# A DeltaNet plus MLP-mixer kernel: the value loads of units 6 to 23 go from SyncE's queue to GpSimd's

## The chip, the cores and the metric

The kernel runs on one core of a Trainium2 chip. The metric is the device time of one execution in microseconds (us). PE is TensorE, DVE is VectorE, ACT is ScalarE, POOL is GpSimd and SP is SyncE, as the profile names them. Every engine works through its own instructions in the order in which the program lists them; a DMA is issued by an instruction on one engine's stream, and what stands behind that instruction on that engine waits until it has been issued.

## What is computed

```python
# DeltaNet, for each of B=4 batches and H=8 heads, S=768 steps, D=48
k_n = k / (norm(k) + 1e-6)
for t in range(S):
    y[t]  = q[t] @ state
    v_old = state @ k_n[t]
    state = state + beta[t] * outer(k_n[t], v[t] - v_old)
x = y.transpose(0, 2, 1, 3).reshape(4, 768, 384)
# MLP mixer
h = relu(x.T @ w_tok1) @ w_tok2
u = x + h.T
out = u + relu(u @ w_ch1) @ w_ch2
```

## The kernel before, in words

The sequence of a batch is cut into 6 units of 128 steps, so there are 24 units (0 to 23, six to a batch), and each unit into two chunks of 64 steps. The recurrence is solved chunk by chunk. All eight heads of a unit are worked on together; in the stacked tiles the 128 partitions hold 64 steps of two heads that are processed side by side, and the free axis holds four such pairs, two chunks and 48 values.

For a unit `u` these jobs do the work. `load_kq(u)` (L372) loads keys and queries. `prep(u)` (L453) takes the norms of the keys, turns keys and queries, and makes two scaled tiles: `mb` (L497), the mask times the scale of every step, and the key columns of `gm` (L514); for the units from 4 on POOL makes both. `grams(u, cc)` (L434) multiplies keys with keys and queries on PE, and DVE scales the result with `mb` (L443). `to_parts`, `invert`, `from_parts` and `join` invert the triangular blocks. From unit 6 on the blocks go out to memory and back by DMA (L608, L655, L685, L633), and the inversion is a long run of small DVE operations (L661, L666). `load_v(u)` (L406) loads the values in four DMAs through `stacked` (L397), and POOL then adds a small constant to the norms (L411) and multiplies the values by them (L414), in place in tile `v_st`. `recur(t)` (L773) walks the chunks `t = 2u` and `2u + 1` in order: DVE subtracts the values from what the state gives (L797, the first and usually the only reader of `v_st`; in the first chunk of a batch PE reads `v_st` itself, L814), and the state is updated. `mixer(b)` (L979) runs the two MLPs of a batch on PE. Weights come in pieces through `round_weights` (L262): a DMA on SP (L271), two operations on ACT, one on DVE, and an addition on POOL (L284) that ends the use of one of three landing buffers `d64`.

Tile `v_st` has two buffers. A load of a new unit's values can start only when the earlier unit in its buffer has been read by L797 for the last time. In the order of the work, unit 6 takes the buffer of unit 5, unit 7 that of 4, unit 8 that of 6, unit 11 that of 9, unit 13 that of 12, unit 16 that of 14, unit 19 that of 18, unit 21 that of 19, unit 22 that of 20 and unit 23 that of 21.

The order of everything is written out by hand: a long string (from L1162) names the jobs step by step, and each word advances one job by one step, whichever engine that step uses. So `v8*2` issues two of the four loads of unit 8 at that place. The string fixes the order on each engine. Each of the four loads of a unit is a step of its own; the fifth step is L411 with L414. Read along the string, the POOL work and the value loads around five units stand in this order, where `v8.1` is the first load of unit 8, `w` an addition of L284, `mb` and `gm` L497 and L514 of a unit, and `V` L411 with L414:

- v7.1 v7.2 v7.3, w15, w4, w19, v6.1 to v6.4, V6, v7.4, w12
- w20, v8.1 v8.2 v8.3, gm12, v8.4, mb13, gm13, V8
- gm14, v11.1 v11.2 v11.3, mb15, gm15, v11.4, mb16, V11
- gm16, v14.1 to v14.4, v13.1 to v13.4, V13, mb18, gm18, V14
- mb21, v16.3 v16.4, V16, gm21 (v16.1 and v16.2 stand before gm20)
- V18, v19.1 to v19.4, V19, v21.1 to v21.4, V21, gm22, v22.1 to v22.4, v23.1, V22, v23.2 v23.3 v23.4, V23

Before the change the loads in these lists are issued by SP and the rest is POOL's; SP meets the loads between its other DMAs of keys, queries, weights, inversion blocks and results. Every DMA of the kernel is issued by SP.

Of the kernel before, what the change touches and what calls it, by code (L numbers as in the profile page):

```python
# [23 lines left out]
def kernel(  # L24
# [39 lines left out]
    nc = tc.nc  # L64
# [5 lines left out]
    NCH = S // U  # L70
# [142 lines left out]
    def place(u):  # L213
        return NV + u if u < 2 else (u - 2) % NV
# [101 lines left out]
    while rounds[-1][-1] < NU - 1:  # L316
        u = rounds[-1][-1] + 1
# [17 lines left out]
    def heads_of(src, u):  # L335

        b, c = divmod(u, NCH)
        return src[b, :, c * U : (c + 1) * U, :].rearrange(
            "(p par) (cc s) d -> par cc s p d", par=2, s=C
        )  # L340
# [31 lines left out]
    def load_kq(u):  # L372
        b, c = divmod(u, NCH)
        kst = kst_of[slot(u)]
        if u >= TU:
            yield from load_rows(u, 0, k)
            assert last_in(u) in ranked
            yield from stacked(kst, k, u)
            yield from load_rows(u, 1, q)
            return  # L380
        for pad, src in ((kpad, k), (qpad, q)):
            assert last_in(u) is None or (pad is kpad, last_in(u)) in turned
            nc.sync.dma_start(
                out=pad[slot(u)][:, :, 0:D],
                in_=src[b, :, c * U : (c + 1) * U, :].rearrange("h t d -> t h d"),
            )
            yield
            if src is k and u >= RU:
                yield from stacked(kst, k, u)

        heads = kpad[slot(u)].rearrange("t (p par) d -> t p par d", par=2)
        for cc in range(2 if u < RU else 0):
            for par in range(2):
                nc.scalar.copy(kst[PAR[par ^ cc], :, cc], heads[PAR[cc], :, par, 0:D])
                yield

    def stacked(dst, src, u):  # L397
        rows = heads_of(src, u)
        for par in range(2):
            for cc in range(2):  # L400
                nc.sync.dma_start(
                    out=dst[PAR[par ^ cc], :, cc], in_=rows[par, cc]
                )
                yield

    def load_v(u):  # L406
        vsts[u] = v_st = loads.tile([128, NP, 2, D], FP32, name="v_st")
        yield from stacked(v_st, v, u)
        assert u in masked
        nrm = nrms[place(u)]  # L410
        nc.gpsimd.tensor_tensor(  # L411
            out=nrm, in0=nrm, in1=eps[:, :, None].to_broadcast([128, NP, 2]), op=ALU.add
        )
        nc.gpsimd.tensor_tensor(  # L414
            out=v_st, in0=v_st,
            in1=nrm[:, :, :, None].to_broadcast([128, NP, 2, D]), op=ALU.mult,
        )
        scaled.add(u)
        yield
# [712 lines left out]
    for u in range(NU):  # L1132
        jobs[f"k{u}"] = load_kq(u)
        jobs[f"p{u}"] = prep(u)
        jobs[f"c{u}"], jobs[f"d{u}"] = (grams(u, cc) for cc in range(2))
        jobs[f"t{u}"] = to_parts(u)
        if u < NCH:
            jobs[f"h{u}"] = join_16(u)
        jobs[f"f{u}"] = from_parts(u)
        jobs[f"j{u}"] = join(u)  # L1140
        jobs[f"v{u}"] = load_v(u)
# [137 lines left out]
```

## Time and profile before

| what | us |
|---|---|
| median of 3 runs (639.05 to 644.09) | 641.08 |
| the profiled execution | 638.03 |
| its span in the profile | 636.3 |
| its mean granted TensorE clock, of full speed | 0.981 |
| DMA traffic read and written | 39.42 MB and 9.44 MB |

The profile is one execution. The times in its rows count from the start of the span, so 1.7 us of the profiled execution's 638.03 us lie outside it. A row of the timeline gives the start, the duration, the engine, the line of the kernel, the operation, what it writes and reads, and in brackets how long the engine had been idle before it and what ended that idle time. `SPq` is SP's queue of issues: its duration is the time in which SP was busy with issuing.

### The profile page before, as it was taken

What the parts mean: (1) busy time and instruction counts of PE and PEld (TensorE: products, weight loads), DVE (VectorE), ACT (ScalarE), POOL (GpSimd) and SP (SyncE); (2) the same over time, 40 slices, a digit from 0 to 9 for tenths busy, and PEclk for the clock granted to TensorE, in tenths of its full rate; (3) what the DMA queues carried; (4) which work ended last, traced back from release to release, by engine and by line L of the source; (5) the groups of instructions that cost most, each with busy time, mean ns of one, the idle gap of its engine ahead of it and who ended that gap; (6) DMA issues with size and microseconds to landing.
All of it is one profiled execution on the core that took longest, in us unless ns stands there. A gap on an engine that the chain in (4) does not pass through costs nothing.

```text
span 636.3 us, 21488 instructions
## 1 busy us (share of the span) xinstructions
PE 606.3 (95%) x9132; PEld 529.0 (83%) x9132; DVE 447.3 (70%) x1132; ACT 259.5 (41%) x631; POOL 108.7 (17%) x146
## 2 busy tenths in 40 slices
PE   8488798899999999999999999999999999999997
PEld 5367676667898988958999999769999987999997
DVE  4987876966899568988969987785627253373643
ACT  7758886447422242125623333135244230223240
POOL 2348364235301113021110010101010000000000
PEclk9878997899999999999999999999999999999999
DMA  9787568646442444354444033202020000000000
GB/s 201 131 145 170 138 133 206 151 111 155 104 111 60 92 110 92 81 131 79 92 103 101 13 94 49 66 10 38 2 54 2 27 2 0 26 1 26 1 26 26
DMA packets 135776, 50.27 MB, mean 79 GB/s; under 512 B 114656, under 2 KB 130144, under 8 KB 135680
## 3 DMA queue, kind: packets, MB, share of 16 engines
q1 hardware_dynamic: 135680, 48.89, 34.5%
q8 instruction: 72, 1.18, 0.8%
q14 instruction: 24, 0.20, 0.1%
HBM read 39.42 MB, written 9.44 MB: 77 GB/s over the span
## 4 chain that ended last, share of the span: by engine, by line
PE 81%; DVE 7%; ACT 5%; DMA 3%; issue 2%; SPq 1%; POOL 0%; DVEq 0%; ACTq 0%; POOLq 0%
PE p_o L1088 26%; PE p_r L958 19%; PE p_c L1066 7%; PE p L986 5%; PE p_h L999 5%; PE p_k L790 3%; PE p_s L828 3%; PE p_g L440 3%; PE p_y L810 3%; DMA d<-in_moe_w_ch_dram 1%; PE p_z L748 1%; PE p_ut L1009 1%; PE p_w L814 1%; DVE sub L661 1%; PE p_y L829 1%
## 5 line engine op out<-in xcount | busy, mean ns | idle before, releaser
L1088 PE MATMUL p_o<-wc,r 128*128 128x192 f32 x720 | 125.8, 329 | 0.6 <-ACT u_t L1013 0.6
L1088 PEld LDWEIGHTS p_o<-wc,r 128*128 128x128 f32 x720 | 116.7, 190 | 2.7 <-ACT u_t L1013 1.1
L970 DVE TENSOR_TENSOR r<-r,p_r 128x512 f32<-128x512 f32 x90 | 59.7, 684 | 39.9 <-PE p_r L958 38.8
L1017 DVE TENSOR_TENSOR xb<-xb,p_o 128x192 f32<-128x192 f32 x84 | 29.3, 350 | 59.5 <-PE p_o L1088 59.3
L967 ACT COPY r<-p_r 128x512 f32<-128x512 f32 x54 | 31.5, 584 | 91.4 <-PE p_r L958 89.8
L666 DVE TENSOR_TENSOR x<-x,sub 128x84 f32<-128x84 f32 (+24 forms) x178 | 59.6, 335 | 6.1
L661 DVE TENSOR_TENSOR sub<-x 128x84 f32<-128x84 f32 (+24 forms) x178 | 58.4, 328 | 7.1 <-DMA x<-n_dram 2.8
L1066 PE MATMUL p_c<-u_t,wc 128*128 128x256 f32 x216 | 51.2, 387 | 0.2 <-ACT u_t L1013 0.2
L1088 PE MATMUL p_o<-wc,s 128*128 128x192 f32 x288 | 50.5, 329 | 0.3 <-DVE xb L1017 0.3
L414 POOL TENSOR_TENSOR v_st<-v_st,nrm 128x384 f32<-128x384 f32 x24 | 20.6, 859 | 174.6 <-DMA v_st<-in_v_dram 140.7
L1088 PEld LDWEIGHTS p_o<-wc,s 128*128 128x128 f32 x288 | 46.8, 190 | 1.2 <-DVE xb L1017 0.6
L820 ACT COPY w_t<-p_w 128x192 f32<-128x192 f32 x48 | 15.3, 319 | 73.2 <-PE p_w L814 72.5
L1066 PEld LDWEIGHTS p_c<-u_t,wc 128*128 128x128 f32 x216 | 39.6, 190 | 5.9 <-ACT u_t L1013 0.4
L974 ACT ACTIVATE r<-r 128x512 f32<-128x512 f32 x54 | 33.8, 630 | 25.6 <-DVE r L970 25.3
L440 PE MATMUL p_g<-kq 48*64 48x128 f32 (+1 forms) x704 | 38.3, 290 | 3.3 <-ACT kq L509 3.3
L497 POOL TENSOR_TENSOR mb<-mask_c,cs 128x512 f32<-128x512 f32 x20 | 21.0, 1050 | 114.1 <-DVE gm L443 45.1
L842 ACT ACTIVATE xb<-p_y 64x192 f32<-64x192 f32 x96 | 31.1, 324 | 21.3 <-PE p_y L829 10.5
L958 PE MATMUL p_r<-u_t,wc 128*128 128x128 f32 x288 | 38.5, 277 | 0.0
L958 PE MATMUL p_r<-t_d,wc 128*128 128x128 f32 x288 | 37.2, 280 | 0.0
L443 DVE TENSOR_TENSOR gm<-p_g,mb 128x512 f32<-128x512 f32 x44 | 29.4, 683 | 10.0 <-PE p_g L440 7.2
L986 PE MATMUL p<-xb,w 128*128 128x384 f32 x96 | 35.6, 513 | 0.0
L958 PEld LDWEIGHTS p_r<-u_t,wc 128*128 128x128 f32 x288 | 35.3, 192 | 0.3
(177 smaller groups left out, 1200.1 us busy)
## 6 DMA issues: line engine op xcount, KB each, us to landing
d<-in_moe_w_ch_dram SPq DMA_DIRECT2D x24, 384.0 KB, 3.9
v_st<-in_v_dram SPq DMA_DIRECT2D x96, 48.0 KB, 2.5
out_dram<-xb SPq DMA_DIRECT2D x23, 192.0 KB, 1.9
kst<-in_k_dram SPq DMA_DIRECT2D x64, 48.0 KB, 3.2
n_dram<-gm SPq DMA_DIRECT2D x72, 32.0 KB, 2.4
pads<-in_k_dram SPq DMA_DIRECT2D x24, 96.0 KB, 2.4
pads<-in_q_dram SPq DMA_DIRECT2D x24, 96.0 KB, 2.5
gm<-w_dram SPq DMA_DIRECT2D x72, 32.0 KB, 2.1
```

The lines of the kernel that those rows point to most:

```text
L440: nc.tensor.matmul(p_g[PAR[i ^ cc], p], kqt[f, p, cc, 0], kqt[f, p, cc])
L661: nc.vector.tensor_tensor(out=tmp, in0=y[:, :, 0:s, s : s + 1].to_broadcast([n, k, s, w]), in1=y[:, :, s : s + 1, s + 1 : m].to_broadcast( ...
L666: nc.vector.tensor_tensor(out=y[:, :, 0:s, s + 1 : m], in0=y[:, :, 0:s, s + 1 : m], in1=tmp, op=ALU.add,)
L842: nc.scalar.mul(y[:, :, D * i : D * i + D], p_y[PAR[1 - i]], 1.0 if c else -1.0)
L958: nc.tensor.matmul(p[:, i], pieces[i // width][:, at : at + 128], f[f"u{n}"], start=first and i == 0, stop=True, skip_group_check=True,)
L967: nc.scalar.copy(o, p)
L970: nc.vector.tensor_tensor(out=o, in0=o, in1=p, op=ALU.add if sign > 0 else ALU.subtract)
L974: nc.scalar.activation(o, o, ACTF.Relu)
L986: nc.tensor.matmul(p_1[dh], piece_of(w1, c, 0)[:, dh * 128 : (dh + 1) * 128], xb[:, c], start=(c == 0), stop=(c == NCH - 1),)
L999: nc.tensor.matmul(p_h, piece_of(w2, j, c * 128)[:, c * 128 : (c + 1) * 128], r1[j], start=(j == 0), stop=(j == NDH - 1),)
L1066: nc.tensor.matmul(p_c[:, k], piece_of(wc1, cb, f * 128)[:, f * 128 : (f + 1) * 128], u_t[:, cb], start=(cb == 0), stop=(cb == NCB - 1),)
L1088: nc.tensor.matmul(p, a[:, m], wc2[:, m, j], start=(start and i == 0), stop=(i == NM - 1), skip_group_check=True,)
```

## The change

The helper that issues the four loads takes the queue as an argument, and `load_v` passes GpSimd's for the units from 6 on (`NCH` is 6). Keys keep SyncE. The order string is unchanged.

```diff
-    def stacked(dst, src, u):
+    def stacked(dst, src, u, queue=nc.sync):
         rows = heads_of(src, u)
         for par in range(2):
             for cc in range(2):
-                nc.sync.dma_start(
+                queue.dma_start(
                     out=dst[PAR[par ^ cc], :, cc], in_=rows[par, cc]
                 )
                 yield
 
     def load_v(u):
         vsts[u] = v_st = loads.tile([128, NP, 2, D], FP32, name="v_st")
-        yield from stacked(v_st, v, u)
+        yield from stacked(v_st, v, u, nc.sync if u < NCH else nc.gpsimd)
```

That is 18 units with four loads each, 72 of the kernel's 96 value loads. One load moves 48 KB: for 64 steps and four heads 256 rows of 48 values (192 bytes) each, from memory into 64 partitions.

## The prediction

> **What bounds the kernel now.** I read the page's busy times and its chain first, then busy time by stretch, then the waits of SP.
>
> ```profile
> PE 606.3 (95%) x9132; PEld 529.0 (83%) x9132; DVE 447.3 (70%) x1132; ACT 259.5 (41%) x631; POOL 108.7 (17%) x146
> PE 81%; DVE 7%; ACT 5%; DMA 3%; issue 2%; SPq 1%; POOL 0%; DVEq 0%; ACTq 0%; POOLq 0%
> ```
>
> ```profile
> core 0: us, PE busy (x) PEld busy (x) DVE busy (x) ACT busy (x) POOL busy (x), PEclk, DMA share, GB/s
> 105.00:140.00 35.00, 33.00 (x421) 21.94 (x422) 30.37 (x83) 13.74 (x36) 8.27 (x10) 0.92 0.59 136
> 140.00:500.00 360.00, 358.86 (x5790) 317.28 (x5784) 274.27 (x703) 131.29 (x321) 49.77 (x67) 1.00 0.33 74
> ```
>
> ```profile
> 105.59 1.31 SPq L401 DMA_DIRECT2D v_st<-in_v_dram  x2
> ```
>
> TensorE is the bound: 81% of the chain is PE's and SP's queue holds 1%. The first moved load is the second of these two issues, at 106 us; the last of all starts at 471 us (the row of L401 below). In 140 to 500 us PE is busy for 358.86 of 360 us, at full granted clock. So a gain on SP has little to be spent on. Its upper bound is the idle time there, 1.1 us, plus idle time (2.0) and lost clock (0.08 of 35, 2.8 us) in 105 to 140 us: 5.9 us, 0.9% of the time. A loss has no such bound: PE runs in a fixed order, and values or masks that come late stop it.
>
> **What the change removes from SP.**
>
> ```profile
> L401 SPq DMA_DIRECT2D v_st<-in_v_dram x96: 595/610/2146, 9.1 to 471.0; - x96
> ```
>
> ```profile
> SPq L401 <- DVE rest L797: 14.8, 2, 14.6
> SPq L271 <- POOL wc L284: 8.4, 5, 3.5
> ```
>
> 72 issues of 0.61 us (the median) are 44 us of SP's time, and 14.8 us in which SP stood before a load until the buffer of `v_st` was free. I cost this at nothing: what waits behind are loads for units and weights to come, and PE is busy meanwhile. If that cover were thinner, it would be the 5.9 us above.
>
> **What it adds to POOL.** POOL gets 72 issues. No row shows what one costs there, since POOL issues no DMA before the change. The nearest rows:
>
> ```profile
> L411 POOL TENSOR_TENSOR nrm<-nrm,eps 128x8 f32<-128x8 f32 x24 | 6.2, 257 | 0.2
> L541 POOL MEMSET z<- 128x2304 f32 x1 | 2.0, 2017 | 0.0
> ```
>
> From below: POOL's shortest work takes about 0.26 us (L411), if all it does is hand the DMA on. From above: if POOL writes the transfer out row by row, four words for each of 256 rows on each of two sides make 2048 words; at the memset's 2017 ns for 2304 elements, 0.88 ns each, that is 1.8 us, and with SP's 0.61 us as the fixed part 2.4 us. The count of four words is my assumption. If besides POOL could write only while DVE is idle (85.73 of 360 us in 140 to 500), an issue of 0.61 us would stretch to 0.61 / 0.238 = 2.6 us, and both together would go beyond 3. I call the cost of one issue d and take d = 1.2 us, twice SP's row for the same transfer and nearer to that row than to any other; the ends 0.26 and 3.0 are kept for the range. At 1.2 us the issues add 86 us to POOL's 108.7 us of work: room enough in total.
>
> The Trainium skill (DMA: Bandwidth & Descriptors, section Latency and other measured facts) gives the first byte at about 1 us through GpSimd and about 0.6 us through SP; by that difference alone an estimate of d is 1.0, and the sum below would be the same, zero. No run here shows it yet.
>
> **Which POOL work gets late.** The loads are put in POOL's own order, so what counts is each later instruction against its first use. POOL's rows, then DVE's:
>
> ```profile
> 111.14 0.83 POOL L414 TENSOR_TENSOR v_st<-v_st,nrm 128x384 f32<-128x384 f32 x1 [6.62 <-DMA lent<-in_k_dram]
> 113.86 1.03 POOL L284 TENSOR_TENSOR wc<-w_f,d 128x384 uint32<-128x384 uint32 x1 [1.90 <-ACT gm L739]
> 139.36 1.04 POOL L497 TENSOR_TENSOR mb<-mask_c,cs 128x512 f32<-128x512 f32 x1
> 158.88 1.02 POOL L284 TENSOR_TENSOR wc<-w_f,d 128x384 uint32<-128x384 uint32 x1 [2.22 <-DVE w_f L280]
> 159.86 0.83 POOL L514 TENSOR_TENSOR gm<-kst,cs 128x384 f32<-128x384 f32 x1
> 163.77 1.04 POOL L497 TENSOR_TENSOR mb<-mask_c,cs 128x512 f32<-128x512 f32 x1 [3.08 <-DVE cs L476]
> 216.47 1.04 POOL L497 TENSOR_TENSOR mb<-mask_c,cs 128x512 f32<-128x512 f32 x1 [18.46 <-DVE gm L443]
> 318.80 1.04 POOL L497 TENSOR_TENSOR mb<-mask_c,cs 128x512 f32<-128x512 f32 x1 [7.98 <-DVE gm L443]
> 326.49 0.83 POOL L414 TENSOR_TENSOR v_st<-v_st,nrm 128x384 f32<-128x384 f32 x1 [6.49 <-DMA v_st<-in_v_dram]
> 412.10 0.83 POOL L414 TENSOR_TENSOR v_st<-v_st,nrm 128x384 f32<-128x384 f32 x1 [11.57 <-DMA v_st<-in_v_dram]
> 470.81 0.83 POOL L414 TENSOR_TENSOR v_st<-v_st,nrm 128x384 f32<-128x384 f32 x1 [38.13 <-DMA v_st<-in_v_dram]
> ```
>
> ```profile
> 169.81 1.27 DVE L443 TENSOR_TENSOR gm<-p_g,mb 128x512 f32<-128x512 f32 x2
> 173.62 0.35 DVE L797 TENSOR_TENSOR rest<-p_k,v_st 128x192 f32<-128x192 f32 x1
> 214.87 0.32 DVE L797 TENSOR_TENSOR rest<-p_k,v_st 128x192 f32<-128x192 f32 x1
> 227.38 0.69 DVE L443 TENSOR_TENSOR gm<-p_g,mb 128x512 f32<-128x512 f32 x1 [0.42 <-PE p_g L440]
> 273.63 0.35 DVE L797 TENSOR_TENSOR rest<-p_k,v_st 128x192 f32<-128x192 f32 x1
> 285.66 0.36 DVE L797 TENSOR_TENSOR rest<-p_k,v_st 128x192 f32<-128x192 f32 x1
> 327.35 0.36 DVE L797 TENSOR_TENSOR rest<-p_k,v_st 128x192 f32<-128x192 f32 x1 [0.75 <-POOL v_st L414]
> 406.68 0.36 DVE L797 TENSOR_TENSOR rest<-p_k,v_st 128x192 f32<-128x192 f32 x1
> 417.93 0.31 DVE L797 TENSOR_TENSOR rest<-p_k,v_st 128x192 f32<-128x192 f32 x1
> 467.61 0.36 DVE L797 TENSOR_TENSOR rest<-p_k,v_st 128x192 f32<-128x192 f32 x1 [0.74 <-PE p_k L790]
> 474.13 0.36 DVE L797 TENSOR_TENSOR rest<-p_k,v_st 128x192 f32<-128x192 f32 x1 [0.98 <-PE p_k L790]
> ```
>
> ```profile
> v_st<-in_v_dram SPq DMA_DIRECT2D x96, 48.0 KB, 2.5
> ```
>
> A load lands 2.5 us after its issue begins; for one that takes d to issue I use 1.9 + d.
>
> - Unit 13's mask. POOL is free at 159.90 us (L284), then come three issues, L514, one issue and L497: it ends at 159.9 + 4d + 1.9 = 161.8 + 4d. First use is 169.81: safe up to d = 2.0.
> - Unit 19's values. Their buffer is free at 407.04 (end of L797). The fourth load starts 3d later and lands at 408.9 + 4d, L414 adds 0.8: 409.7 + 4d against 417.93, safe up to d = 2.0. At d = 1.2 they are 1.6 us later than now, within the 5.0 us between 412.93 and 417.93.
> - Unit 13's values, in the same way from 273.98: 276.7 + 4d against 285.66, d = 2.2.
> - Unit 16's values have no slack today: ready at 327.32, used at 327.35 after 0.75 us of DVE idle time. Two loads now follow unit 21's mask (ends at 319.84): 322.6 + 2d, at d = 1.2 2.3 us earlier than today; later than today only from d = 2.4. Gain on DVE 0.75 us, on the busy PE nothing.
> - Unit 15's mask stands behind three loads of unit 11, whose buffer is free at 215.19 (end of L797 at 214.87): 216.2 + 3d against 227.38, d = 3.7.
> - Unit 23's first load takes POOL's place for over 20 us, until 467.97, with unit 22's L414 behind it. That still ends at 469.0 + d plus 0.2, against a first use at 474.13.
> - The weight addition at 113.86 now follows three loads that start when unit 5's L414 ends, at about 112.0: it starts at 112.0 + 3d, 1.7 us late at d = 1.2. SP waits for its end today before it issues a further weight load (its waits on L284 above), so SP and the key and query loads behind it move by those 1.7 us, less what SP saves on three issues. What is loaded there serves units 11 and 12, whose masks come at 139.36 us and later.
>
> The sum at d = 1.2: nothing is added to PE's path and nothing taken. The profiled execution's 638.03 us stay; it lies 3.05 us below the median of 641.08, and the forecast is for a median: **641 us**.
>
> **Rivals.**
>
> *An issue is dear (slower).* Place: the stretches above; price by their terms; it decides from d = 2.0. At 2.4 us: unit 13's mask is 1.6 late, unit 19's values 1.4, unit 13's values 0.6, together 3.6 us, 645. At 3.0 us: 4.0, 3.8 and 3.0 us, plus unit 16 with 1.2 against its first use and 2.2 us for unit 8 (its L414 stands behind the late mask and two more POOL steps, about 2.0 us, and ends at 163.8 + 4d against 173.62): 14 us, 655. For it: 256 short rows each. Against it: POOL's software does not make it slow elsewhere: L497 takes 1.04 us for the 128x512 elements for which DVE's L443 takes 0.69.
>
> The Trainium skill (SBUF — State Buffer, section SBUF: two separate sides) says that a DMA issued by GpSimd starves while DVE holds the port pair that both share, and gives (section A bandwidth-pool intuition that's wrong) 620 ns alone and 3100 ns beside a DVE copy. As an estimate by that figure d would be 3.1, and this rival's price a little above 14 us. The same page (Who interferes with whom) ties this to DVE's copies and tensor-scalar forms; whether its starving comes in here, no run yet shows.
>
> *DVE is held (slower).* POOL's work already slows DVE:
>
> ```profile
> 411.38 0.39 DVE L666 TENSOR_TENSOR x<-x,sub 64x234 f32<-64x234 f32 x1
> 412.25 0.94 DVE L666 TENSOR_TENSOR x<-x,sub 64x238 f32<-64x238 f32 x1
> ```
>
> The second ran beside L414 at 412.10 and took 0.55 us more. If each of 72 issues does this, DVE loses up to 40 us; DVE's idle time in 140 to 500 us is 85.73 us, so a good part goes unseen. I put a quarter of it on the path: 10 us, 651.
>
> *SP's relief pays (faster).* The earlier loads feed PE's idle time and lift the clock in 105 to 140 us: at most 5.9 us, 635. Against it: at the first moved loads PE is idle for 2.0 of 35 us, and the work before 106 us keeps its queue.
>
> **How the numbers follow.** No change 0.45 (641, own range 638 to 645); dear issue 0.33; DVE held 0.14; relief 0.08. A measurement of this kernel can tell about 1% from no change, 6.4 us. The dear issue stays within that in 0.03, DVE held in 0.01 and relief in 0.03: faster 0.05, same 0.45 + 0.07 = 0.52, slower 0.43. The range goes from 636.5 (most of the relief) to 657 (issues of 3.0 us and a little more); outside lie about 0.03 below, and above 0.12 of the dear issue and 0.03 of DVE held.
>
> **What would show it.** POOL's rows: 72 issues of about 1.2 us; 2.0 or more speaks for the first rival. Unit 13's L443 still near 169.8 and unit 19's L797 near 417.9: right; PE idle there, waiting for L414 or L443: wrong. The longer forms of L661 and L666 at more than 0.4 us beside issues speak for the second rival; PE's clock above 0.92 in 105 to 140 us for the third. The forecast is wrong if PE's busy share of 140 to 500 us falls by more than 6 us.

## The result, and the profile after

| | median us | runs | lowest to highest |
|---|---|---|---|
| before | 641.12 | 20 | 637.66 to 645.17 |
| after | 644.82 | 20 | 639.92 to 650.62 |

The ratio is 1.0045, with a 95% interval of 1.0024 to 1.0066. The changed kernel is 3.7 us by the medians, 2.9 by the ratio, slower; little, but clear of zero. The forecast of no change (641) lies inside the measured spread but outside the interval: something was lost that the prediction priced at nothing.

Two of the 20 runs after, 649.81 us and the first profiled execution with 650.62 us, lie more than 1.5% above the fastest and are left out of the ratio. All rows "after" below are of a second profiled execution of the same kernel (`again`, 646.12 us, span 644.4). The first has the same three stops of PE: it is busy for 17.53, 37.33 and 38.67 us of the last three stretches shown below.

What answers to the bound first: the page's busy times, then busy time by stretch. After the start and the length of a stretch stand the busy time and instruction count of PE, PE's loads, DVE, ACT and POOL, the granted clock, the DMA share and the traffic.

```profile
PE 611.8 (95%) x9132; PEld 531.2 (82%) x9132; DVE 451.1 (70%) x1132; ACT 259.8 (40%) x631; POOL 153.1 (24%) x218
...
PE 75%; DVE 11%; ACT 4%; DMA 4%; issue 3%; SPq 3%; POOL 1%; DVEq 0%; ACTq 0%; POOLq 0%
```

```profile
105.00:140.00 35.00, 32.89 (x403) 21.60 (x402) 30.75 (x84) 13.59 (x35) 12.34 (x18) 0.90 0.59 136
140.00:500.00 360.00, 354.27 (x5740) 311.31 (x5739) 276.26 (x698) 131.76 (x321) 89.94 (x132) 1.00 0.33 75
```

PE's share of the chain falls from 81% to 75%, DVE's rises from 7% to 11%, and in 140 to 500 us PE is busy for 354.27 us instead of 358.86. The 4.6 us that are missing lie in a few places. The same view in shorter stretches, before and then after:

```profile
140.00:180.00 40.00, 39.31 (x848) 33.39 (x842) 30.61 (x73) 24.06 (x61) 15.13 (x18) 1.00 0.58 138
180.00:200.00 20.00, 20.00 (x160) 17.91 (x159) 18.79 (x51) 2.71 (x5) 3.21 (x6) 1.00 0.43 100
260.00:300.00 40.00, 40.00 (x641) 30.68 (x639) 35.27 (x99) 12.81 (x34) 5.43 (x7) 1.00 0.38 89
300.00:340.00 40.00, 39.60 (x778) 37.09 (x773) 32.02 (x80) 15.73 (x39) 5.67 (x8) 1.00 0.48 105
```

```profile
140.00:180.00 40.00, 38.83 (x829) 32.31 (x828) 27.56 (x65) 23.24 (x57) 20.44 (x26) 0.96 0.57 130
180.00:200.00 20.00, 18.43 (x167) 16.29 (x166) 16.22 (x46) 2.57 (x7) 6.46 (x10) 1.00 0.40 102
260.00:300.00 40.00, 38.46 (x507) 29.04 (x507) 35.92 (x103) 9.45 (x27) 6.32 (x10) 1.00 0.37 86
300.00:340.00 40.00, 38.59 (x886) 36.08 (x883) 33.66 (x70) 19.15 (x48) 13.03 (x19) 1.00 0.44 92
```

Three stops of PE, of 1.57, 1.54 and 1.01 us, make 4.1 of the 4.6 us. They are called by their place in the first profile of the kernel before, near 182, 282 and 325 us; in `again` they end at 186.94, 288.89 and 333.71 us. The 0.5 us in 140 to 180 us are no loss of the change: two more profiles of the kernel before have 38.73 and 39.11 us there. Nor is the shift of some 3 us with which the rows after 160 us begin: in the same two profiles the L443 of 169.81 us stands at 174.26 and 173.21.

The issues themselves are cheap. The first row is POOL's group by line (count, then busy us and mean ns, then idle time and its releasers); the others are of the DMA view (packets, MB, share of the DMA engines; KB each, median us from issue to landing).

```profile
L401 POOL DMA_DIRECT2D v_st<-in_v_dram x72 | 44.9, 630 | 118.0 <-DVE rest L797 53.0 <-DVE sub L661 44.7 <-DVE t_c L927 15.9
```

```profile
q0 software_dynamic: 2304, 3.54, 3.0%
...
v_st<-in_v_dram POOLq DMA_DIRECT2D x72, 48.0 KB, 2.7
```

An issue takes 0.63 us on POOL, against 0.61 on SP, and lands after 2.7 us, against 2.5.

**The stop near 282 us.** POOL, then DVE, after:

```profile
279.67 2.46 POOL L401 DMA_DIRECT2D v_st<-in_v_dram  x4 [22.04 <-DVE sub L661]
...
284.58 0.83 POOL L414 TENSOR_TENSOR v_st<-v_st,nrm 128x384 f32<-128x384 f32 x1 [2.23 <-DMA v_st<-in_v_dram]
285.37 1.07 POOL L497 TENSOR_TENSOR mb<-mask_c,cs 128x512 f32<-128x512 f32 x1
286.40 0.83 POOL L514 TENSOR_TENSOR gm<-kst,cs 128x384 f32<-128x384 f32 x1
...
287.47 0.83 POOL L414 TENSOR_TENSOR v_st<-v_st,nrm 128x384 f32<-128x384 f32 x1
```

```profile
281.05 0.36 DVE L666 TENSOR_TENSOR x<-x,sub 128x198 f32<-128x198 f32 x1
...
284.63 0.91 DVE L666 TENSOR_TENSOR x<-x,sub 128x108 f32<-128x108 f32 x1
285.57 0.97 DVE L661 TENSOR_TENSOR sub<-x 128x84 f32<-128x84 f32 x1
286.58 0.75 DVE L666 TENSOR_TENSOR x<-x,sub 128x84 f32<-128x84 f32 x1
```

and the same place before:

```profile
282.07 0.83 POOL L414 TENSOR_TENSOR v_st<-v_st,nrm 128x384 f32<-128x384 f32 x1 [28.28 <-DMA v_st<-in_v_dram]
```

```profile
275.96 0.37 DVE L666 TENSOR_TENSOR x<-x,sub 128x198 f32<-128x198 f32 x1
...
279.52 0.27 DVE L666 TENSOR_TENSOR x<-x,sub 128x108 f32<-128x108 f32 x1
279.83 0.25 DVE L661 TENSOR_TENSOR sub<-x 128x84 f32<-128x84 f32 x1
...
281.48 0.21 DVE L666 TENSOR_TENSOR x<-x,sub 128x30 f32<-128x30 f32 x1
```

Beside the four issues of POOL (279.67 to 282.13 us) DVE runs at its usual pace: the 128x198 form takes 0.36 us, before 0.37. Beside the four arithmetic steps it does not: 0.91 and 0.97 us instead of 0.27 and 0.25. Before, POOL began these steps at 282.07, after the inversion's last operation (281.48 and 0.21), because unit 13's values had landed only then. SP had come to their loads at 277.72 us, 3.7 us after L797 had freed the buffer (273.98); POOL comes to them 0.6 us after the same L797 (279.08). Now they land while the inversion still runs. A load that arrives sooner has let POOL's arithmetic in beside DVE's, and PE waits for what stands behind it on DVE (`[1.54 <-DVE xb L1003]` at PE's next L999).

DVE operations that read one input from PSUM are not held: over the whole of `again` L443, which reads `p_g`, takes 0.65 to 0.69 us, and L797, which reads `p_k`, 0.31 to 0.36 us, beside POOL's arithmetic or not.

The Trainium skill (SBUF — State Buffer, section Who interferes with whom) says that a DVE instruction with two inputs in SBUF contends with a GpSimd instruction that reads SBUF, and not with one that only writes there. The rows above agree with the first half (0.91 us against 0.27). No run here tests the second half: no row shows whether POOL reads or writes SBUF while it issues a DMA.

**The stop near 325 us** is of the same kind: unit 16's L414 and unit 21's L514 stand beside the weight forms of L927.

```profile
330.18 0.85 POOL L414 TENSOR_TENSOR v_st<-v_st,nrm 128x384 f32<-128x384 f32 x1 [1.86 <-DMA v_st<-in_v_dram]
330.99 0.88 POOL L514 TENSOR_TENSOR gm<-kst,cs 128x384 f32<-128x384 f32 x1
```

```profile
330.06 0.28 DVE L927 TENSOR_TENSOR t_c<-u_t,t_c 128x128 f32<-128x128 f32 x1
330.26 0.91 DVE L927 TENSOR_TENSOR t_d<-t_d,u_t 128x128 f32<-128x128 f32 x1
331.10 0.91 DVE L927 TENSOR_TENSOR t_d<-u_t 128x128 f32<-128x128 f32 x1
```

**The stop near 182 us** is another thing: DVE waits for the blocks of the next inversion, which go to memory by the writes of L608 and come back by the read of L655. After:

```profile
186.21 0.19 DVE L661 TENSOR_TENSOR sub<-x 128x30 f32<-128x30 f32 x1 [2.67 <-DMA x<-n_dram]
```

and before:

```profile
180.16 0.20 DVE L661 TENSOR_TENSOR sub<-x 128x30 f32<-128x30 f32 x1
```

Before, there was no wait, but no slack either: the read had landed at 179.96 us.

### The profile page after: what moved, and what is told of

It reads as the page before. It is cut to its first block, busy times and chain, and to the rows that moved or that the text cites. A ratio compares the mean times of both kernels' runs of the same rounds, so it can differ in the third digit from the quotient of the medians.

```text
span 648.8 us, 21509 instructions
## 1 busy us (share of the span) xinstructions
PE 615.4 (95%) x9132; PEld 534.5 (82%) x9132; DVE 452.2 (70%) x1132; ACT 259.7 (40%) x631; POOL 152.2 (23%) x218
## 3 DMA queue, kind: packets, MB, share of 16 engines
q0 software_dynamic: 2304, 3.54, 2.8%
HBM read 39.42 MB, written 9.44 MB: 75 GB/s over the span
## 4 chain that ended last, share of the span: by engine, by line
PE 73%; DVE 12%; DMA 6%; ACT 4%; issue 3%; SPq 1%; POOL 1%; DVEq 0%; POOLq 0%; ACTq 0%
PE p_o L1088 22%; PE p_r L958 20%; PE p_c L1066 7%; PE p_h L999 5%; PE p L986 3%; PE p_k L790 3%; DVE x L666 3%; DVE sub L661 3%; PE p_s L828 3%; PE p_y L810 3%; PE p_g L440 3%; DMA x<-n_dram 2%; DMA n_dram<-gm 1%; PE p_z L748 1%; PE p_w L814 1%
## 5 line engine op out<-in xcount | busy, mean ns | idle before, releaser
L1088 PE MATMUL p_o<-wc,r 128*128 128x192 f32 x720 | 127.9, 332 | 3.9 <-DVE xb L1017 3.3
L401 POOL DMA_DIRECT2D v_st<-in_v_dram x72 | 44.6, 626 | 119.7 <-DVE rest L797 52.0
L661 DVE TENSOR_TENSOR sub<-x 128x84 f32<-128x84 f32 (+24 forms) x178 | 60.9, 342 | 12.4 <-DMA x<-n_dram 8.1
L666 DVE TENSOR_TENSOR x<-x,sub 128x84 f32<-128x84 f32 (+24 forms) x178 | 60.7, 341 | 6.1
L820 ACT COPY w_t<-p_w 128x192 f32<-128x192 f32 x48 | 15.2, 317 | 80.9 <-PE p_w L814 80.1
L497 POOL TENSOR_TENSOR mb<-mask_c,cs 128x512 f32<-128x512 f32 x20 | 21.1, 1053 | 95.8 <-DVE cs L476 35.7
L999 PE MATMUL p_h<-r,w 128*128 128x384 f32 x96 | 34.1, 508 | 1.9 <-DVE xb L1003 1.9
L443 DVE TENSOR_TENSOR gm<-p_g,mb 128x512 f32<-128x512 f32 x44 | 29.3, 681 | 8.9 <-PE p_g L440 7.3
```

What stands on the lines that cost most here:

```text
L401: queue.dma_start(out=dst[PAR[par ^ cc], :, cc], in_=rows[par, cc])
L661: nc.vector.tensor_tensor(out=tmp, in0=y[:, :, 0:s, s : s + 1].to_broadcast([n, k, s, w]), in1=y[:, :, s : s + 1, s + 1 : m].to_broadcast( ...
L666: nc.vector.tensor_tensor(out=y[:, :, 0:s, s + 1 : m], in0=y[:, :, 0:s, s + 1 : m], in1=tmp, op=ALU.add,)
L999: nc.tensor.matmul(p_h, piece_of(w2, j, c * 128)[:, c * 128 : (c + 1) * 128], r1[j], start=(j == 0), stop=(j == NDH - 1),)
L1088: nc.tensor.matmul(p, a[:, m], wc2[:, m, j], start=(start and i == 0), stop=(i == NM - 1), skip_group_check=True,)
```

## The experiments

Except where a diff is shown, a kernel is the changed one with another condition in the one line of `load_v`:

```diff
-        yield from stacked(v_st, v, u, nc.sync if u < NCH else nc.gpsimd)
+        yield from stacked(v_st, v, u, nc.sync if u < NCH or u in (9, 10) else nc.gpsimd)
```

`sp_` names the units that go back to SP, `pool_` those that alone are POOL's. `again` is the changed kernel, `before_2` and `before_3` are the kernel before. Ratios are to the kernel before on the same chip, of 12 runs each (`twice` 6), with 95% intervals. The profiled execution of `pool_6_10` took 648.95 us, the longest of its twelve. PE's busy time is of the profiled execution; "wait" is that of the first L661 after L655 near 182 us.

| kernel | wait | PE 180-200 | PE 260-300 | PE 300-340 | ratio, interval |
|---|---|---|---|---|---|
| before | 0 | 20.00 | 40.00 | 39.60 | |
| `before_2` | 0.31 | 20.00 | 40.00 | 39.44 | 1.0003, 0.9974 to 1.0031 |
| `before_3` | 1.21 | 19.91 | 40.00 | 39.42 | one run |
| `again` | 2.67 | 18.43 | 38.46 | 38.59 | 1.0046, 1.0016 to 1.0077 |
| `sp_9_10` | 4.14 | 17.00 | 37.73 | 39.28 | 1.0044, 1.0015 to 1.0073 |
| `sp_13_14` | 0.93 | 19.96 | 40.00 | 38.54 | 1.0031, 1.0000 to 1.0062 |
| `sp_9_10_13_14` | 3.82 | 17.33 | 40.00 | 38.97 | 1.0030, 1.0003 to 1.0056 |
| `sp_13_14_16` | 5.00 | 16.15 | 40.00 | 39.50 | 1.0015, 0.9982 to 1.0049 |
| `sp_6_8` | 2.13 | 19.02 | 38.60 | 39.28 | 1.0045, 1.0011 to 1.0079 |
| `sp_6_8_b` | 2.33 | 18.83 | 39.28 | 39.01 | one run |
| `pool_6_10` | 5.21 | 15.93 | 40.00 | 39.09 | 1.0011, 0.9981 to 1.0041 |
| `pool_13_14` | 2.18 | 18.97 | 39.73 | 39.12 | 1.0022, 0.9988 to 1.0056 |
| `pool_13_14_b` | 2.06 | 19.08 | 38.73 | 39.60 | one run |
| `pool_17_23` | 0.15 | 19.95 | 40.00 | 39.40 | 0.9996, 0.9964 to 1.0028 |
| `k14_pool` | 0.59 | 19.80 | 39.26 | 38.86 | 1.0023, 0.9999 to 1.0048 |
| `k14_pool_sp_13_14_16` | 0.53 | 19.80 | 40.00 | 39.48 | 0.9995, 0.9975 to 1.0014 |
| `twice` | 0 | 20.00 | 40.00 | 39.60 | 1.0078, 1.0054 to 1.0101 |

PE's busy time is not the whole price of the longest stops. Where PE is busy for 15.93 and 16.15 of the 20 us (`pool_6_10`, `sp_13_14_16`), the granted clock of that stretch is 0.83, and it is 0.91 at 17.33 us (`sp_9_10_13_14`), where `again` and `sp_9_10` have 1.00.

Two names of theories recur with another meaning from set to set; each expectation says what it means by them.

**First set: which loads make the stops near 182 and 282 us.**

> The changed kernel once more, for a second trace. Theory ROUND TRIP: taken out of SP's order, the value loads run earlier than the inversion blocks that units 10 to 17 send to memory and read back; they compete with these DMAs, DVE starts rounds 3 and 4 of the inversion late, and some of POOL's arithmetic on the values now falls into an inversion and holds DVE. Then this trace shows again: L661 idle for the landing of x<-n_dram by 2 us or more near 185 us, PE idle near 187 and near 290 us, at least three operations of L661/L666 in 285 to 295 us at 0.7 us and more, and a time about 0.45% above the kernel before (643 to 646 us). Rival STRAY: these waits belong to one disturbed execution; then PE is busy in 180 to 300 us for 119 us of 120 and the extra time lies elsewhere. Rival ISSUE: the issues themselves (0.63 us each) hold POOL or DVE; then L661/L666 are longer beside issues of L401 on POOL and mask or value steps end late.

> The loads of units 9 and 10 go back to SP, 64 of the 72 stay on POOL. ROUND TRIP: the wait of L661 for x<-n_dram near 185 us is gone (under 0.5 us) and with it the stop of PE there; the time falls by 2 to 4 us against the changed kernel, the stop near 290 us stays. ISSUE: 8 of 72 issues are gone, the time falls by at most 0.5 us. STRAY: no change that can be told.

> The loads of units 13 and 14 go back to SP. ROUND TRIP: the wait of L661 for x<-n_dram near 264 us and the long L661/L666 at the end of that inversion (near 288 us) are gone, PE does not stop there; the time falls by 2 to 4 us against the changed kernel, the stop near 187 us stays. ISSUE: at most 0.5 us less. STRAY: no change that can be told.

> The loads of units 9, 10, 13 and 14 go back to SP, 56 stay on POOL. ROUND TRIP: both stops of PE are gone, the time is that of the kernel before within 0.3% (639 to 643 us). ISSUE: 16 of 72 issues are gone, so about a fifth of the loss: some 0.3% above the kernel before is left.

The loss is there again (1.0046), and so are the stops, so STRAY fails. Taking units 13 and 14 off POOL removes the stop near 282 us in both kernels that do it (40.00 of 40 us). In `sp_13_14` POOL starts unit 13's L414 after the inversion's end again:

```profile
285.39 0.83 POOL L414 TENSOR_TENSOR v_st<-v_st,nrm 128x384 f32<-128x384 f32 x1 [31.92 <-PE p_h L999]
```

```profile
284.39 0.21 DVE L666 TENSOR_TENSOR x<-x,sub 128x30 f32<-128x30 f32 x1
```

Taking off units 9 and 10, whose loads POOL issues beside the blocks' way through memory, does not remove the stop near 182 us (4.14 and 3.82 us of waiting). So those loads are not its cause, and ROUND TRIP fails for this stop. It fails in `sp_13_14` too, where the stop should have stayed: the wait there is only 0.93 us and PE is busy 19.96 of 20 us, though none of the loads put back is issued before 250 us. Why is not known. The times of single stops, 1 to 2 us, are within the intervals, so here the windows decide, not the ratios.

**Second set: one part alone, and unit 16.**

> The kernel before once more, unchanged: a second profiled execution of it. It is there for the stop near 182 us, where the inversion's first subtraction (L661) waits for its blocks from memory. Theory FETCH: that round trip ends on time or 2 to 3 us late according to how 16 KB instruction packets fall on its writes, in any version, so it can be late here too (busy time of PE in 180 to 200 us of 17 to 20). Theory STRAY: it is late only where values are loaded by POOL, so PE is busy 20.0 of 20 here as in the first profile of the kernel before. Both: 260 to 300 us 40.0 busy, 300 to 340 us 39.5 or more. Ratio to the kernel before 1.000 with an interval of about 0.003 on either side, which is also the noise of the other comparisons.

> Only the loads of units 13 and 14 by GpSimd, all others by SyncE. Theory COLLISION: these loads alone bring the stop near 282 us, because their values land before the inversion's end and the multiplications of L414 then run beside its last steps: L661 and L666 there 0.7 us or more instead of 0.25, busy time of PE in 260 to 300 us of 38 or less, in 300 to 340 us 39.5 as before; time 1 to 3 us over the kernel before. Rival SP AHEAD (the stop needs SP to be free of the other loads): 40.0 of 40 and no change of time. Near 182 us: 20.0 busy by STRAY, anything from 17 to 20 by FETCH.

> Only the loads of units 6 to 10 by GpSimd, 11 to 23 by SyncE. COLLISION: no stop near 282 us (40.0 of 40) and none near 325 us (39.5 of 40 in 300 to 340 us); the rival SP AHEAD says the same here, since SP has 11 to 23 again. Near 182 us: STRAY expects the stop as in four of five kernels with values on POOL (17 to 18.5 of 20 in 180 to 200 us) and a time 2 us over the kernel before; FETCH leaves it open, 17 to 20.

> The change without units 13, 14 and 16, whose loads stay on SyncE. COLLISION: the stop near 282 us is gone (40.0 of 40 in 260 to 300 us) as in the kernel without 13 and 14, and so is the one near 325 us (the forms of L927 are not held, 39.5 of 40 in 300 to 340 us), because unit 16's multiplication comes later again; what is left over the kernel before is the stop near 182 us, 0 to 2.5 us. Rival: unit 21's columns (L514), not unit 16's values, hold the forms, and the time from 300 to 340 us stays at 38.5 to 39.0.

`sp_13_14_16` shows what makes the stop near 325 us: with unit 16 on SP, PE is busy 39.50 of 40 us, and L927 is never held, because unit 16's L414 comes after the forms:

```profile
333.73 1.12 POOL L414 TENSOR_TENSOR v_st<-v_st,nrm 128x384 f32<-128x384 f32 x1 [6.17 <-DMA v_st<-in_v_dram]
```

```profile
330.95 0.28 DVE L927 TENSOR_TENSOR t_d<-u_t 128x128 f32<-128x128 f32 x1
```

The other profiles agree. In the eight with unit 16 on POOL (`twice` aside, where L417 comes after the forms) one or two forms of L927 take 0.91 or 0.92 us; in the nine with unit 16 on SP none does. PE loses most where two forms are held (busy 38.54 to 38.67 of 40 us; 38.86 to 39.28 with one). `pool_6_10` and `pool_13_14` were expected at 39.5 of 40 us here and have 39.09 and 39.12, without a form held; PE waits there for ACT's L820 (0.4 us).

`pool_13_14` is the other half of the proof for 282 us: these eight loads alone bring the collision.

```profile
283.20 0.93 POOL L414 TENSOR_TENSOR v_st<-v_st,nrm 128x384 f32<-128x384 f32 x1 [2.88 <-DMA v_st<-in_v_dram]
```

```profile
283.48 0.73 DVE L661 TENSOR_TENSOR sub<-x 128x58 f32<-128x58 f32 x1
284.24 0.97 DVE L666 TENSOR_TENSOR x<-x,sub 128x58 f32<-128x58 f32 x1
```

It comes one step later in the inversion, holds fewer operations, and costs PE 0.27 us, in the second profile (`pool_13_14_b`) 1.27: less than the 2 us or more expected. How many of the last steps are caught differs from one profile to the next. `pool_6_10` has no stop near 282 us, as expected. Near 182 us it has the longest wait of all, 5.21 us, and yet `pool_13_14`, which issues nothing on POOL until 256 us, waits 2.18 us there. That does not fit STRAY, which expected no stop in `pool_13_14`; FETCH, which allowed anything, is not tested by it.

**Third set: slack for the round trip, and twice the issues.** In `k14_pool` POOL also issues the four key loads of unit 14, which SP issued between the nine writes of blocks:

```diff
-                yield from stacked(kst, k, u)
+                yield from stacked(kst, k, u, nc.gpsimd if u == 14 else nc.sync)
```

The same edit stands at the other place where these loads are issued. In `twice` each load on POOL is cut into two halves of its pairs:

```diff
-                queue.dma_start(
-                    out=dst[PAR[par ^ cc], :, cc], in_=rows[par, cc]
-                )
+                for h in range(2 if queue is nc.gpsimd else 1):
+                    n = NP // 2 if queue is nc.gpsimd else NP
+                    queue.dma_start(
+                        out=dst[PAR[par ^ cc], h * n : h * n + n, cc],
+                        in_=rows[par, cc][:, h * n : h * n + n],
+                    )
```

> The change, and in addition the four loads of unit 14's keys by GpSimd, which SyncE issued between the nine writes of inversion blocks before the read of L655. Theory SLACK: the stop near 182 us comes from a round trip (writes of the blocks, read by L655) that has no slack, and without four issues of 0.6 us SyncE sends the last write up to 2.4 us sooner, so L661 waits for x 0 to 1.5 us instead of 2.7 to 5.2, PE is busy over 19.5 of 20 us from 180 to 200 us, and the time falls 1 to 3 us below the changed kernel's (about 642). Rival: the writes are not held by SyncE's issues but by the transfers themselves, then L661 still waits over 2 us, PE is busy 16 to 18.5 us there, and the time stays at 644. The stops near 282 and 325 us stay in both (260 to 300 us: 37 to 38.5 of 40).

> The same with the values of units 13, 14 and 16 back on SyncE. SLACK and COLLISION together: all three stops gone, PE busy as in the kernel before in every window from 140 to 500 us (0.6 us lost or less from 180 to 340 us), ratio to the kernel before 1.000 give or take 0.002. Since PE then has no more work taken away than before, neither theory expects it to be faster than the kernel before. Rival (some cost is spread over the whole of the kernel, such as POOL's issues): the windows are as before and the ratio is still 1.003 or more.

> The change with each of POOL's 72 loads cut into two of half the size (144 issues, the same bytes). Theory CHEAP: issuing is not what the change costs; if an issue's time goes by its rows, a half load takes about 0.3 us and nothing changes, if it is a fixed time, POOL issues 44 us more, still beside other work for the most part; time within 1.5 us of the changed kernel's 644. Theory DEAR (the time lost is POOL's issuing): twice the issues bring about twice the loss, 647 us or more.

`k14_pool` bears SLACK out: the wait falls to 0.59 us and PE is busy 19.80 of 20 us; its ratio of 1.0023 lies between the two kernels and is told from neither. The stop near 282 us is smaller than expected (39.26 of 40 us). With 13, 14 and 16 back on SP as well, all three stops are gone and so is the loss: 0.9995, below the whole interval of the changed kernel. Sixty loads of values and four of keys are then still POOL's, so no cost spread over the issues is left to be seen. As expected it is not faster than the kernel before.

`twice` came out between its two theories, at 646.31 us. An issue does not get shorter with its rows:

```profile
L403 POOL DMA_DIRECT2D v_st<-in_v_dram x144 | 84.9, 604 | 104.2 <-DVE sub L664 39.2 <-DVE rest L800 35.0 <-issue 30.0
```

From 180 us on its windows are full. Ahead of that PE is idle in two places for longer than in the kernel before: 2.3 us in 140 to 180 us (37.74 of 40 us busy; three profiles before 0.7 to 1.3) and 3.7 us in 105 to 140 us (31.35 of 35 us busy; before 1.7 to 2.3).

The first place is near 176 us. There the issues have pushed POOL's L500 (the mask, L497 of the other kernels) and L517 in beside DVE's L299 and L1043 (three lines longer for the edit):

```profile
170.13 1.06 POOL L500 TENSOR_TENSOR mb<-mask_c,cs 128x512 f32<-128x512 f32 x1
...
173.62 0.89 POOL L517 TENSOR_TENSOR gm<-kst,cs 128x384 f32<-128x384 f32 x1 [2.42 <-PE p_y L832]
```

```profile
170.24 1.57 DVE L299 TENSOR_TENSOR wc<-wc 128x192 f32<-128x192 f32 x2
...
173.73 1.18 DVE L1043 TENSOR_TENSOR r<-r 128x384 f32<-128x384 f32 x1
```

The same two groups take 0.70 and 0.55 us where POOL does no arithmetic. The second place is near 118 us. Two of POOL's weight additions, which now stand behind six half loads, run back to back beside DVE's L669, which takes 0.40 us alone:

```profile
117.97 1.02 POOL L284 TENSOR_TENSOR wc<-w_f,d 128x384 uint32<-128x384 uint32 x1
```

```profile
117.41 1.85 DVE L669 TENSOR_TENSOR x<-x,sub 128x228 f32<-128x228 f32 x1
```

PE waits 1.97 us for L800, the next operation on DVE. This place is not peculiar to the doubled issues: in `k14_pool` the same pair of additions holds L666 for 2.06 us and PE waits 2.86 us, and in the three profiles of the kernel before L666 takes 1.08 or 1.09 us there and PE waits up to 1.30. In both places the mechanism is again POOL's arithmetic beside DVE's, near 176 us shifted by the issues. No wait of PE in the trace of `twice` is put down to a DMA that POOL issues.

**Last set: what lengthens the round trip.**

> A third profiled execution of the kernel before, for the wait of the first L661 after the read of L655 near 180 us: none and 0.31 us in the first two, 0.6 to 5.2 us in the profiles with loads of values on GpSimd. STRAY (the round trip is longer only where GpSimd issues loads): 0.3 us or less. FETCH (it varies by execution in any version): anything from 0 to 5 us.

> The change without units 6 to 8, whose loads stay on SyncE (9 to 23 by GpSimd). If the loads of units 6 to 8 lengthen the round trip near 182 us (NEAR LOADS), L661 waits 0 to 1.2 us there as in the kernel before, and the time falls by about 2 us to 642. If it varies by execution whatever is near (FETCH), anything from 0 to 5 us. The stops near 282 and 325 us stay (37 to 38.5 of 40 us, and 38.5 to 39 of 40).

> The same kernel again, for a second profile of the wait near 182 us: by NEAR LOADS 0 to 1.2 us in both, by FETCH anything from 0 to 5 us, and the two profiles may differ.

> Only units 13 and 14 by GpSimd, a second profile. By NEAR LOADS the wait near 182 us is that of the kernel before, 0 to 1.2 us, and the 2.2 us of the first profile were chance; by a cause that goes with the program as a whole it is about 2 us again. Near 283 us two or three operations of L661 and L666 held for 0.4 to 0.7 us each, as in the first.

> Only units 17 to 23 by GpSimd, all loads before 330 us by SyncE. NEAR LOADS: the wait near 182 us is 0 to 1.2 us. COLLISION: no stop near 282 us and none near 325 us (40.0 of 40, 39.5 of 40), and since the late units stand beside no inversion that PE waits for, the time is that of the kernel before within 0.2 per cent.

NEAR LOADS fails as the only cause: without units 6 to 8 the wait is 2.13 and 2.33 us, with 13 and 14 alone it is 2.06 again. That both repeats agree with their first profiles speaks against chance, but the kernel before itself varies (0, 0.31 and 1.21 us, where STRAY allowed 0.3). `pool_17_23` waits 0.15 us, has no stop and costs nothing that twelve runs can tell (0.9996, 0.9964 to 1.0028): these are 28 of the 72 moved loads.

The traces show at which link the trip gets longer. SP's last writes and the read, before and in `pool_13_14`:

```profile
171.81 3.43 SPq L608 DMA_DIRECT2D n_dram<-gm  x5
176.47 0.34 SPq L655 DMA_DIRECT2D x<-n_dram  x1
```

```profile
173.36 3.45 SPq L608 DMA_DIRECT2D n_dram<-gm  x5
...
179.78 0.34 SPq L655 DMA_DIRECT2D x<-n_dram  x1
```

From the end of the last issue (start plus duration) to L655 it is 1.23 us before and 2.97 in `pool_13_14`. It is 1.22 to 1.23 in all three profiles of the kernel before and in `pool_17_23`, 1.92 in `sp_13_14`, and 2.75 to 3.14 in the other ten with loads on POOL, `k14` and `twice` aside. In those three it is 1.55 (`k14_pool`), 2.55 (`k14_pool_sp_13_14_16`) and 3.06 (`twice`), and the trip still ends in time: in the first two the last write is issued about 2 us sooner against PE than in the kernel before, and in `twice` DVE itself comes later, after the stop near 176 us. The DMA view of 5 us around it (busy tenths in 40 slices of 0.125 us, traffic by slice, packets of instructions) shows what happens, before from 173.3 us and in `pool_13_14` from 174 us:

```profile
DMA  1840011000007701760186000004000005896499
GB/s 31 138 73 4 4 7 8 9 4 0 0 16 124 110 12 23 133 102 5 24 136 96 7 0 0 0 0 131 0 0 0 0 0 197 197 328 197 164 492 393
...
q8 instruction: 1, 0.02, 1.2%
```

```profile
DMA  1565950001000017601860185029400000000010
GB/s 32 88 131 109 169 79 8 5 7 9 11 10 13 2 22 128 105 8 25 132 99 7 31 145 82 4 35 265 74 3 0 0 0 0 0 0 0 2 7 7
...
q8 instruction: 1, 0.02, 1.7%
```

Before, the writes end at 176.2 us (slice 23), an instruction packet (a DMA packet that the profile labels `instruction`) passes by itself (131 GB/s in one slice, 176.7 us), and then the data of the read move. In `pool_13_14` the packet falls among the last writes (265 GB/s, 177.4 us); all but a few writes are done by 177.7, and the rest, 16 packets of 128 bytes, come 0.9 us later (2, 7, 7 GB/s from 178.6 us on). Such late packets, 16 to 32 of them and 0.4 to 1.1 us behind the others, are in each of the ten profiles with the long gap and in none of the five without it (three of the kernel before, `pool_17_23`, `sp_13_14`). That the late packets stand behind the instruction packet on one DMA engine is argued from this, not shown: an instruction packet of 16 KB takes 0.9 us or more in these traces, and no run moves it by itself. Why the last writes come 0.8 to 1.3 us later against PE in these kernels, and so meet it, stays open; so does why the read itself lands after 4.1 to 6.1 us instead of 3.5 to 4.7 in most kernels with units 6 to 8 on POOL. What is shown is the place, and that with four fewer issues of SP ahead of it the wait is 0.59 and 0.53 us, in both kernels that have this.

## Why the prediction failed where it did

- **PE bounds the kernel, SP's relief is worth nothing: right.** 44 us of issues left SP and no version got faster. But "I cost this at nothing" also meant that no loss could come from SP's side, and the bound given beside it was for a gain only. The round trip through L608 and L655 has no slack in the kernel before (L661 starts with no wait, in two more profiles after 0.31 and 1.21 us). That chain was never checked, and it costs about 1.6 us in `again`; why it gets longer with the change stays open.
- **The price of an issue: right in kind, too high.** d is 0.63 us, near SP's row, not 1.2; the largest is 0.78 us. The rival of dear issues is refuted. (Its lower bound was misread: L411 with 0.26 us is not POOL's shortest work, a MEMSET of L1263 takes 0.10 us. Nothing hung on it.) The 3100 ns beside a DVE copy of the Trainium skill (SBUF — State Buffer, section A bandwidth-pool intuition that's wrong) are not seen in any run here; in `again` all but one of the DVE operations beside an issue are TENSOR_TENSOR, STREAM_TRANSPOSE or TENSOR_REDUCE, so the case that the Trainium skill describes there hardly arises. Twice the issues at 0.60 us each do lose more, but at the two places found POOL's arithmetic holds DVE.
- **The check of each POOL step against its first use: the step that failed.** The deadlines in the list hold, as the prediction said: unit 13's L443 starts at 173.02 us, 3.2 later than in the first profile of the kernel before and sooner than in the two others. What the list never asks is whether a step that comes *earlier* meets another engine. For unit 13's values it says 276.7 + 4d against 285.66, safe; for unit 16's, 2.3 us earlier and "on the busy PE nothing". These two are the places of the stops near 282 and 325 us: what was put at nothing cost about 1.5 and 1.0 us of PE's time, since POOL's arithmetic, moved earlier, holds DVE's operations of 0.25 to 0.28 us to 0.91 and 0.97.
- **The rival that DVE is held: the right contact, the wrong agent.** Its row, L666 held beside L414, was the mechanism that came true. It was priced with 72 issues, which do not hold DVE (0.36 us beside them against 0.37), and not with the arithmetic steps that the change moves.
- **SP's relief does not pay.** From 105 to 140 us PE is busy for 32.89 us at a clock of 0.90, where it was 33.00 at 0.92.
- **The sum.** 4.1 us of PE's time in one profile, against 2.9 to 3.7 us in the medians. No experiment resolves a single stop in the median; together they are resolved (1.0046 against 0.9995).

## What to carry to other kernels

Where a load is moved to a faster queue, list what its landing releases, and look at what the neighbouring engine runs at that earlier moment: a late load can be the only thing that keeps two engines apart. An engine that is idle for the most part still costs the critical path when its arithmetic overlaps DVE's operations with two inputs in SBUF. Before a reordering is costed at nothing, look for chains through memory whose reader starts without a wait, since they have no slack to give.

## What the runs showed of the hardware

- A DMA of 48 KB in 256 rows takes POOL 0.63 us to issue, one of half the rows 0.60: the time goes by the issue, not by its rows.
- On POOL's queue the 72 loads move in 2304 packets for 3.54 MB, 32 to a load: 16 of 3072 bytes and 16 of 4 bytes. On SP's queue the same loads move in 256 packets of 192 bytes each, beside 16 of 4 bytes. The landing is no sooner for it (2.7 us against 2.5).
- In the rows above, DVE operations with both inputs in SBUF take up to 0.7 us longer beside one or two POOL operations on such inputs (0.97 us instead of 0.25), and up to 1.7 us longer beside two that run back to back (2.06 us instead of 0.40, `k14_pool`). Beside a DMA that POOL issues they take no longer (0.36 us against 0.37), and those with one input in PSUM take no longer beside either (L797 at most 0.36 us in `again`).
